# Summing the last 512 rows of w4 in four rows of 256 columns, with finer last loads and the output on another load semaphore

## The chip, the cores, the metric

The kernel runs on one core of a Trainium2 chip. The metric is the device time of one execution in microseconds (us). All quoted runs are "fast"; for a single core that only says that no run was over 1.5% above the fastest of its kernel. Times inside an execution are counted from its first instruction. The span of a profiled execution is about 1.8 us shorter than its time.

Engine names: PE is TensorE, DVE VectorE, ACT ScalarE, and SyncE issues most loads. PEld is PE's weight load.

## The reference

One decode step: grouped-query attention over a long cache plus a small gated MLP, in parallel, summed.

```python
# x: (1, 1, 1024); k_cache, v_cache: (1, 4, 65536, 128); wq, wo: 1024x4096, 4096x1024
# w1, w2: 1024x1024; w3: 1024x3584; w4: 3584x1024, all bf16
xn = layernorm(x)
A  = attention(xn @ wq, k_cache, v_cache) @ wo
h  = mix(gelu(layernorm(xn) @ w1)) @ w2
B  = xn + h + gelu(layernorm(xn + h) @ w3) @ w4     # S = 1, so the mix is a zero padding here
return x + A + B
```

(In the reference the shift by the mix leaves only zeros for one position, so the kernel feeds w3 from the same normed row.) Nearly all of the work is reading 170 MB.

## The kernel before

Loads go through eight hardware load semaphores in turn. The kernel sums every contribution to the output (x, each group's wo, w2, w4) in one PSUM bank `psB`: columns 0 to 511 in row 0, columns 512 to 1023 in row 32. The two rows lie in two 32-column strips of the PE array, so the two matmuls of a pair run side by side (in the trace they start 4 ns apart). w4 is the last weight; its last chunks are loaded in small pieces.

```python
W4_PIECES = ((8, 8), (8, 2, 1, 1))            # chunks of 128 rows, for the two tiles of w4
...
stream += [("wo", HKV - 1), ("V", NU - 1), ("w4", 0), ("w4", 1)]     # the last loads, in order
...
def row_acc(j, lhsT, rhs):                     # 1x512 into row 32*j of psB
    nc.tensor.matmul(psB[32 * j:32 * j + 1, :], lhsT=lhsT, rhs=rhs, start=False, stop=False,
                     tile_position=(0, 32 * j), skip_group_check=True)
...
def compute_w4(i, lo=0, hi=None): ...          # for each chunk, row_acc for j = 0 and 1
...
    compute_w4(0, W4_PIECES[0][0])
    compute_w4(1)
    out_t = ppool.tile([64, 512], BF16, name="out_t", tag="p_sb")
    nc.scalar.copy(out=out_t[:], in_=psB[0:64, :])
    nc.scalar.dma_start(out=out[0, 0, :].rearrange("(j n) -> j n", j=2),
                        in_=out_t[:].rearrange("(a b) n -> a b n", b=32)[:, 0, :])
```

## Time and profile before

405.86 us (median of 3, 405.73 to 405.91) when the prediction was made.

| event in the tail | us from the start |
|---|---|
| last V complete | 382.92 |
| w4 in pieces of 8, 8, 8 chunks complete | 387.80, 392.70, 397.59 |
| pieces of 2, 1, 1 chunks complete | 398.83, 399.48, 400.12 |
| last matmul ends | 400.54 |
| output copy on ACT | 400.58 to 401.16 |
| output lands | 402.86 |
| last instruction ends | 404.05 |

A load is complete when the last of the 16 DMA engines has counted up its semaphore; these moments are read from the trace's semaphore records. The table says that everything until 400.12 is the DMA stream, and 3.9 us of serial tail follow.

From the page of the kernel before, the span and, in 40 slices, the busy tenths of PE, the granted PE clock in tenths and the busy tenths of the DMA engines:

```profile
span 404.1 us, 3287 instructions
...
PE   0382727839483859292929394565658561948094
...
PEclk9998558688897979797978979596959895879769
DMA  8999999999999999999999999999999999999993
```

DMA is full from the second slice to the last but one; PE is not. From the chain of waits of the kernel before, its last pieces (start, duration, what):

```profile
355.04 42.55 DMA big<-in_B_w_dram
397.59 0.04 issue
397.63 2.93 PE psB L179 x24
400.56 0.02 issue
400.58 0.58 ACT out_t L526
```

From the timeline of the kernel before (start, duration, engine, line, operation, out<-in, shapes, count, idle before and its releaser):

```profile
397.63 2.91 PE L179 MATMUL psB<-big,cols_h 128*1 128x512 bf16 x24 [1.55 <-DMA big<-in_B_w_dram]
...
400.58 0.58 ACT L526 CAST out_t<-psB 64x512 bf16<-64x512 f32 x1 [25.40 <-PE psB L179]
401.19 0.61 ACTq L527 DMA_DIRECT2D out_dram<-out_t  x1
```

The chain puts the last 2.93 us down to PE, but these 24 matmuls hold one more real wait. PE starts a pair every 0.216 us from 397.63 on, and the small pieces of 2 and 1 chunks are there before it needs them. Only the last pair waits: it starts at 400.16, 0.04 us after the last load.

### The profile page before, as it was taken

To read this page: it belongs to the slowest core of one execution; us is meant where nothing else is said; L and a number is where in the kernel's file an instruction comes from. 1 tells how busy PE (TensorE), PEld (TensorE's weight loads), DVE (VectorE), ACT (ScalarE), POOL (GpSimd) and SP (SyncE) were. 2 spreads that over 40 slices of the span, in tenths; PEclk is the share of its full clock that TensorE was granted. 3 is DMA by queue.
4 is the path that set the end of the run, shared out by engine and by line. 5 is a ranking of instruction groups with operands and counts; after the bars stand their busy time and mean duration, and the time that the engine had idled before them with its cause. 6 is when DMAs were issued, how large, how long until landed. Compare 5 with 4: busy or idle time off the path is not lost.

```text
span 404.1 us, 3287 instructions
## 1 busy us (share of the span) xinstructions
PE 236.2 (58%) x1392; PEld 94.1 (23%) x1392; DVE 211.8 (52%) x241; ACT 34.3 (8%) x61; POOL 6.4 (2%) x19
## 2 busy tenths in 40 slices
PE   0382727839483859292929394565658561948094
PEld 0131202313131323031313231122213220313041
DVE  0310046957658584566585473738393934665310
ACT  1000210110101011001010101010101010010100
POOL 4000100000000000000000000000000000000000
PEclk9998558688897979797978979596959895879769
DMA  8999999999999999999999999999999999999993
GB/s 357 422 415 431 449 416 439 440 418 429 448 417 425 454 409 430 444 431 417 448 428 418 436 420 438 428 444 423 428 436 428 422 436 435 431 426 430 420 427 144
DMA packets 7237, 170.11 MB, mean 421 GB/s; under 512 B 1070, under 2 KB 1074, under 8 KB 1462
## 3 DMA queue, kind: packets, MB, share of 16 engines
q1 hardware_dynamic: 6912, 169.87, 98.1%
q8 instruction: 11, 0.18, 0.2%
q0 software_dynamic: 160, 0.02, 0.0%
q10 hardware_dynamic: 150, 0.01, 0.0%
q14 instruction: 4, 0.03, 0.0%
HBM read 169.88 MB, written 0.01 MB: 420 GB/s over the span
## 4 chain that ended last, share of the span: by engine, by line
DMA 49%; PE 30%; DVE 10%; another core or an unknown queue 6%; ACT 2%; issue 2%; SPq 0%; DVEq 0%; ACTq 0%
DMA big<-in_A_k_cache_dram 35%; PE sc L383 21%; DMA big<-in_B_w_dram 11%; DVE big L372 5%; PE oacc L457 4%; DMA x_bf<-in_A_x_dram 3%; DVE s_sb L390 2%; PE psq L250 1%; ACT p_sb L421 1%; PE psB L179 1%; PE psB L239 1%; DVE pT L424 1%; PE pm_mx L400 1%; DVE og L439 0%
## 5 line engine op out<-in xcount | busy, mean ns | idle before, releaser
L383 PE MATMUL sc<-big,qdiag 128*128 128x512 bf16 x512 | 150.0, 461 | 104.9 <-DVE big L372 104.9
L372 DVE STREAM_TRANSPOSE big<-big 128x2048 f32<-128x2048 f32 x64 | 142.4, 2279 | 49.4 <-DMA big<-in_A_k_cache_dram 49.4
L383 PEld LDWEIGHTS <-qdiag 128*128 128x128 bf16 x512 | 56.8, 111 | 193.2 <-issue 100.3
L457 PE MATMUL oacc<-big,pT 128*32 128x512 bf16 x512 | 37.7, 396 | 9.7 <-DMA big<-in_A_v_cache_dram 9.7
L390 DVE TENSOR_SCALAR_CACHE_REDUCE s_sb<-sc 128x1024 f32<-128x1024 f32 x16 | 19.6, 1225 | 45.0 <-PE sc L383 45.0
L424 DVE STREAM_TRANSPOSE pT<-p_sb 128x1024 bf16<-128x1024 bf16 x16 | 19.8, 1240 | 16.8 <-ACT p_sb L421 16.8
L463 ACT COPY ob<-oacc 128x512 f32<-128x512 f32 x12 | 7.0, 586 | 214.6 <-PE oacc L457 214.6
L421 ACT ACTIVATE p_sb<-s_sb,nball 128x1024 bf16<-128x1024 f32 x16 | 18.4, 1150 | 76.5 <-DVE nball L419 76.5
L457 PEld LDWEIGHTS <-pT 128*32 128x32 bf16 x512 | 14.0, 99 | 28.7 <-issue 17.1
L400 PE MATMUL pm_mx<-ident_f,mx 128*1 128x128 f32 x16 | 4.3, 270 | 16.7 <-DVE s_sb L390 16.7
L419 DVE COPY nball<-pm_mx 128x1 f32<-128x1 f32 x16 | 2.5, 153 | 17.5 <-PE pm_mx L413 17.5
L250 PE MATMUL psh<-big,ln_rep_b 128*32 128x512 bf16 x56 | 5.5, 505 | 8.8 <-DMA big<-in_B_w_dram 8.8
L466 DVE SCALAR_TENSOR_TENSOR og<-oacc,wb,og 128x512 f32<-128x512 f32 x4 | 3.0, 751 | 12.5 <-PE oacc L457 12.5
L179 PE MATMUL psB<-big,cols_h 128*1 128x512 bf16 x56 | 7.7, 420 | 1.6 <-DMA big<-in_B_w_dram 1.6
L189 PE MATMUL pm_ln<-ln_rowsum_a,ones_f 128*128 128x1 f32 x2 | 0.6, 348 | 13.7 <-DVE sel L213 13.7
L179 PE MATMUL psB<-w,oT 128*1 128x512 bf16 x64 | 7.6, 379 | 0.0
L473 PE MATMUL pm_e<-og,selbig 128*128 128x128 f32 x32 | 5.6, 326 | 3.2 <-DVE nball L419 2.3
L402 DVE TENSOR_REDUCE negm<-pm_mx 1x8 f32<-1x128 f32 x16 | 4.4, 275 | 5.4 <-PE pm_mx L400 5.4
L250 PEld LDWEIGHTS <-ln_rep_b 128*32 128x32 bf16 x72 | 3.4, 120 | 15.0 <-issue 12.2
L183 DVE CAST xT<-x_bf 128x8 f32<-128x8 bf16 x1 | 0.2, 172 | 12.0 <-DMA x_bf<-in_A_x_dram 12.0
L400 PEld LDWEIGHTS pm_mx<-ident_f,mx 128*1 128x1 f32 x16 | 1.3, 79 | 21.9 <-DVE s_sb L390 21.9
L439 DVE SCALAR_TENSOR_TENSOR og<-ob,wb,og 128x512 f32<-128x512 f32 x8 | 6.0, 751 | 0.1
(98 smaller groups left out, 80.5 us busy)
## 6 DMA issues: line engine op xcount, KB each, us to landing
big<-in_A_k_cache_dram SPq DMA_DIRECT2D x16, 4096.0 KB, 46.1
big<-in_A_v_cache_dram SPq DMA_DIRECT2D x16, 4096.0 KB, 39.9
big<-in_A_wq_dram SPq DMA_DIRECT2D x2, 4096.0 KB, 16.9
w<-in_A_wo_dram SPq DMA_DIRECT2D x4, 2048.0 KB, 30.1
big<-in_B_w_dram SPq DMA_DIRECT2D x2, 3584.0 KB, 34.3
big<-in_B_w_dram SPq DMA_DIRECT2D x3, 2048.0 KB, 40.7
w<-in_B_w_dram SPq DMA_DIRECT2D x2, 2048.0 KB, 42.6
big<-in_B_w_dram SPq DMA_DIRECT2D x1, 512.0 KB, 43.4
```

Of the source, the lines that this page charges most:

```text
L179: nc.tensor.matmul(psB[32 * j:32 * j + 1, :], lhsT=lhsT, rhs=rhs, start=False, stop=False, tile_position=(0, 32 * j), skip_group_check=True)
L250: nc.tensor.matmul(acc[i][32 * q:32 * q + 32], lhsT=rep[:, c, :], rhs=wt[:, k, 512 * s:512 * (s + 1)], start=first, stop=last, tile_positi ...
L372: nc.vector.transpose(out=words, in_=words)
L383: nc.tensor.matmul(sc[:, sub, :], lhsT=qdiag[:, c0:c0 + P], rhs=cols[:, sub, s, :, b, :, r], start=(s == 0 and b == 0 and r == 0), stop=(s ...
L390: nc.vector.tensor_scalar(out=s_sb[:], in0=sc[:], scalar1=SCALE, scalar2=None, op0=ALU.mult, op1=ALU.max, accum_out=mx[:])
L400: nc.tensor.transpose(pm[0:1, 0:P], unit.pop((u, "mx"))[:, 0:1], ident_f[:])
L421: nc.scalar.activation(out=p_sb[:], in_=unit.pop((u, "ssb"))[:], func=ACTF.Exp, bias=nball[:, b:b + 1], scale=1.0, accum_out=group[(g, "la ...
L424: nc.vector.transpose(out=pT[:].rearrange("p u n -> p (u n)"), in_=p_sb[:].rearrange("p u n -> p (u n)"))
L439: nc.vector.scalar_tensor_tensor(out=og[:], in0=ob[:], scalar=wb[:, k:k + 1], in1=og[:], op0=ALU.mult, op1=ALU.add)
L457: nc.tensor.matmul(oacc[32 * q:32 * (q + 1), :], lhsT=pT[:, sub, 32 * t:32 * (t + 1)], rhs=vt[:, sub, :, t, :], start=(sub == 0 and t < 4) ...
L463: nc.scalar.copy(out=ob[:], in_=oacc[:])
L473: nc.tensor.matmul(pe[:, 0:P], lhsT=selbig[:, cg, :], rhs=og[:, 128 * cg:128 * (cg + 1)], start=(cg == 0), stop=(cg == 3))
```

## The change

The intent: leave less to do after the last load. The sum of all but the last four chunks is copied out of `psB` (DVE), spread by four f32 matmuls with an identity over four rows of 256 columns (`psC`), and the last four chunks are added in four strips. The output copy is then 256 columns wide instead of 512. Loads near the end are split so that PE can start earlier; five more loads also shift the output to the eighth load semaphore, the last one that the end of the program waits for.

```diff
-W4_PIECES = ((8, 8), (8, 2, 1, 1))
+W4_PIECES = ((4, 4, 4, 4), (4, 4, 2, 1, 1))
+LAST = 4
 ...
-                nc.sync.dma_start(out=t[:], in_=wo_v[i] if src is None else src)
+                src = wo_v[i] if src is None else src
+                for lo, hi in ((0, 4), (4, 8)) if it == ("wo", HKV - 1) else ((0, 8),):
+                    nc.sync.dma_start(out=t[:, lo:hi], in_=src[:, lo:hi])
 ...
-                nc.sync.dma_start(out=t[:], in_=src)
+                n = UKEYS // SUBS if it == ("V", NU - 1) else UKEYS
+                for at in range(0, UKEYS, n):
+                    nc.sync.dma_start(out=t[:, at:at + n], in_=src[:, at:at + n])
 ...
+    def close_out():
+        acc = opool.tile([64, 512], F32, name="acc", tag="ob")
+        nc.vector.tensor_copy(out=acc[:], in_=psB[0:64, :])
+        psC = ps_O.tile([P, 512], F32, name="psC", tag="oacc")
+        for j in range(4):
+            nc.tensor.matmul(psC[32 * j:32 * j + 32, 0:256],
+                             lhsT=ident_f[0:64, 32 * (j // 2):32 * (j // 2) + 32],
+                             rhs=acc[:, 256 * (j % 2):256 * (j % 2 + 1)], start=True, stop=False, ...)
+        for k in (the last LAST chunks):
+            for j in range(4):
+                nc.tensor.matmul(psC[32 * j:32 * j + 1, 0:256], lhsT=vals["hT"][:, c:c + 1],
+                                 rhs=wt[:, 1024 * k + 256 * j:1024 * k + 256 * (j + 1)], ...)
+        return psC
 ...
-    compute_w4(1)
-    out_t = ppool.tile([64, 512], BF16, name="out_t", tag="p_sb")
-    nc.scalar.copy(out=out_t[:], in_=psB[0:64, :])
+    compute_w4(1, 0, sum(W4_PIECES[1]) - LAST)
+    psC = close_out()
+    out_t = ppool.tile([P, 256], BF16, name="out_t", tag="p_sb")
+    nc.scalar.copy(out=out_t[:], in_=psC[:, 0:256])
```

(Shortened; the output DMA writes four rows of 256.)

More of the change, by code (lines that the diff above doesn't have):

```diff
@@ L335, in compute_w2, with compute_w4 @@
         st.done(("w2", 0))
-    def compute_w4(i, lo=0, hi=None):
+    def compute_w4(i, lo, hi):
         wt = st.tiles[("w4", i)]
-        c0, n = sum(map(sum, W4_PIECES[:i])), sum(W4_PIECES[i])
-        hi = n if hi is None else hi
+        c0 = sum(map(sum, W4_PIECES[:i]))
         for k in range(lo, hi):
@@ L343, in compute_w4 @@
                 row_acc(j, vals["hT"][:, c0 + k:c0 + k + 1], wt[:, 1024 * k + 512 * j:1024 * k + 512 * (j + 1)])
-        if hi == n:
-            st.done(("w4", i))
+    def close_out():
[3 more added lines that the diff above has]
+        for j in range(4):
+            nc.tensor.matmul(psC[32 * j:32 * j + 32, 0:256], lhsT=ident_f[0:64, 32 * (j // 2):32 * (j // 2) + 32],
+                             rhs=acc[:, 256 * (j % 2):256 * (j % 2 + 1)], start=True, stop=False,
+                             tile_position=(0, 32 * j), skip_group_check=True)
+        wt = st.tiles[("w4", 1)]
+        for k in range(sum(W4_PIECES[1]) - LAST, sum(W4_PIECES[1])):
+            for j in range(4):
+                c = sum(W4_PIECES[0]) + k
+                nc.tensor.matmul(psC[32 * j:32 * j + 1, 0:256], lhsT=vals["hT"][:, c:c + 1],
+                                 rhs=wt[:, 1024 * k + 256 * j:1024 * k + 256 * (j + 1)], start=False, stop=(c == FC - 1),
+                                 tile_position=(0, 32 * j), skip_group_check=True)
+        return psC
     clock = [0]
@@ L451, in compute_v @@
         vt = st.tiles[("V", u)][:].rearrange("p (u s t d) -> p u s t d", u=SUBS, s=SETS, t=16)
-        oacc = ps_O.tile([P, 512], F32, name="oacc")
+        oacc = ps_O.tile([P, 512], F32, name="oacc", tag="oacc")
         pT = unit.pop((u, "pT"))
@@ L517 @@
             compute_v(i)
+    half = sum(W4_PIECES[0]) // 2
     while waiting:
@@ L520 @@
         if waiting:
-            compute_w4(0, 0, W4_PIECES[0][0])
-    compute_w4(0, W4_PIECES[0][0])
-    compute_w4(1)
-    out_t = ppool.tile([64, 512], BF16, name="out_t", tag="p_sb")
-    nc.scalar.copy(out=out_t[:], in_=psB[0:64, :])
-    nc.scalar.dma_start(out=out[0, 0, :].rearrange("(j n) -> j n", j=2),
+            compute_w4(0, 0, half)
+    compute_w4(0, half, 2 * half)
+    compute_w4(1, 0, sum(W4_PIECES[1]) - LAST)
+    psC = close_out()
+    out_t = ppool.tile([P, 256], BF16, name="out_t", tag="p_sb")
+    nc.scalar.copy(out=out_t[:], in_=psC[:, 0:256])
+    nc.scalar.dma_start(out=out[0, 0, :].rearrange("(j n) -> j n", j=4),
                         in_=out_t[:].rearrange("(a b) n -> a b n", b=32)[:, 0, :])
```

## The prediction

> **What bounds the kernel now.** The DMA stream. The page's 40 slices show DMA at 9 tenths from the second slice to the last but one (421 GB/s), while PE is busy 58% and DVE 52% of 404.1 us. The chain of waits ends with one DMA piece of 42.55 us (w4), then PE 2.93 us and ACT 0.58 us. So only the tail after the stream can change, and the stream's own length. In the trace's landing records the last V is complete at 382.92, the three big w4 pieces at 387.80, 392.70, 397.59, the small ones at 398.83, 399.48 and 400.12. After the last landing: two 1x512 matmuls end at 400.54, the 64x512 output copy on ACT takes 0.58 us, the output DMA's issue 0.61 us, it lands at 402.86 (1.69 us after the copy's end), SyncE then steps through five more semaphore waits (0.061 us each) before the end barrier; the span ends at 404.05.
>
> **What the change does, costed.**
> 1. Output semaphore: five more loads shift the output from the third load semaphore waited for to the eighth. The five waits after it disappear: -0.30 us, all on the critical path.
> 2. Output copy 128x256 instead of 64x512. ACT PSUM copies took 258 ns at 128 columns and 586 at 512, so 0.37 us (estimate) for 0.58: -0.21, on the path.
> 3. Five more DMAs. Landing intervals (9.72 us for 4 MB, 4.89 for 2 MB, 0.645 for 256 KB) leave 0.04 to 0.06 us per DMA, so the last landing moves to about 400.3. The late pieces now wait for an earlier load on their semaphore before issue, the last until about 385.5; about 6 MB are then still queued, so the stream doesn't run dry.
> 4. V and wo in halves: the last V's second half needs only 16 matmuls, so the group's end comes about 1.7 us sooner. PE had 1.55 us idle just before 397.63: off the path.
> 5. close_out is new and serial. The last piece before it lands at about 397.8; its eight 1x512 matmuls end near 398.85. DVE copies 64x512 f32 from PSUM: 0.69 us (q_row copy, same width). Then four f32 matmuls of 256 columns, two records each; an f32 record of 512 columns took 0.83 us at half clock, so 0.21 us at full clock. Neighbouring column strips overlapping, five slots: 1.1 us; serial: 1.7 us. The Trainium skill, "TensorEngine Tiling (Array Packing)", Key Properties, says different tiles execute in parallel; the trace agrees for bf16 (pairs of 1x512 matmuls start 4 ns apart), no run shows it for f32. f32 ends near 400.7 (or 401.3), after the last landing. The sixteen 1x256 matmuls wait behind it in order: four groups of 0.11 us and 0.17 us latency, end near 401.3 (401.9), against 400.54 before.
>
> So PE ends +0.75 (to +1.4) later, copy -0.21, waits -0.30: net about +0.25 to +0.9 us. PE's granted clock should be full there [...]; if it is half, another 1 us.
>
> **Prediction:** 406.2 us, 8 in 10 between 405.3 and 406.9. Faster by over 2%: 0.005; within 2%: 0.99; slower: 0.005.
>
> **What would show it right:** the last load landing near 400.3; PE not waiting for the last three pieces but for the DVE copy of psB; f32 matmuls spanning 1.1 to 1.7 us; ACT copy near 0.37 us starting after 401.2; no semaphore waits behind the output's.
>
> **What would make it wrong:** f32 matmuls overlapping fully or much cheaper, so the last landing is again what PE waits for (then about 405.4); an idle or cold PE in the tail; small pieces slowing the stream.

## The result, and the profile after

406.62 us (median of 4, 405.92 to 407.06), beside 405.81 (405.73 to 405.91) for the kernel before. Ratio 1.0018, 95% interval 1.0001 to 1.0036: the same within 2%. A ratio is the mean time of one kernel's fast runs over that of the other's of the same rounds, so it is not quite the ratio of the medians. The profiled run took 406.61 us.

From the page of the changed kernel, the lines that answer to those of before:

```profile
span 404.8 us, 3326 instructions
...
PE   0383526749465767293929384566566762838393
...
PEclk9997759979896969686868988596969695979577
DMA  8999999999999999999999999999999999999993
```

From its chain of waits, the last pieces:

```profile
373.24 24.70 DMA big<-in_B_w_dram
397.94 0.04 issue
397.98 1.05 PE psB L184 x8
399.03 0.02 issue
399.05 0.69 DVE acc L352
399.74 0.14 issue
399.88 0.98 PE psC L355 x8
400.86 0.98 PE psC L362 x16
401.84 0.02 issue
401.86 0.37 ACT out_t L548
```

From its timeline:

```profile
397.98 1.03 PE L184 MATMUL psB<-big,cols_h 128*1 128x512 bf16 x8 [1.46 <-DMA big<-in_B_w_dram]
...
399.05 0.68 DVE L352 COPY acc<-psB 64x512 f32<-64x512 f32 x1 [9.68 <-PE psB L184]
...
399.88 0.98 PE L355 MATMUL psC<-acc,ident_f 64*32 64x256 f32 x8 [0.87 <-DVE acc L352]
...
400.79 1.02 PE L362 MATMUL psC<-big,cols_h 128*1 128x256 bf16 x16
401.86 0.37 ACT L548 CAST out_t<-psC 128x256 bf16<-128x256 f32 x1 [25.98 <-PE psC L362]
402.26 0.62 ACTq L549 DMA_DIRECT2D out_dram<-out_t  x1
```

The DMA piece of the chain now ends at 397.94, not with the last load, which lands at 400.45. After it comes a serial chain: eight matmuls, DVE copy, f32 matmuls, sixteen matmuls. PE's last sixteen no longer wait for any load: they start at 400.79, when the last load has been there for 0.34 us.

The two traces' difference adds up. PE ends at 401.81 instead of 400.54: +1.27. The output copy takes 0.37 instead of 0.58: -0.21. From the output's landing to the end barrier there is one semaphore wait instead of six: -0.31. With +0.02 of small gaps that is +0.77, the difference of the spans (404.05 and 404.82).

The semaphore waits, from SyncE's records (not a view of the profile, but its instruction records: start and end in ns; the first wait of each kernel is for the output):

```
before  402872-402899  402936-402964  402997-403025  403057-403085  403118-403146  403177-403205  then the barrier at 403245
after   403950-403978  then the barrier at 404017
```

One more thing stands in the trace. The matmuls after 400.0 are slow for their size, and the view of windows shows why (window, length, busy us and count of PE, PEld, DVE, ACT, POOL, then the granted clock, DMA share and GB/s); changed kernel:

```profile
396.63:400.04 3.41, 1.19 (x12) 0.45 (x15) 0.68 (x1) 0.00 (x0) 0.00 (x0) 1.00 0.45 170
400.04:403.40 3.36, 1.77 (x24) 0.38 (x16) 0.00 (x0) 0.37 (x1) 0.00 (x0) 0.50 0.00 0
```

At 400.04 the clock fell to half, in the middle of the f32 matmuls, after a window in which PE had been busy for 1.19 of 3.41 us. In the trace of the kernel before, the window at this place holds more matmul work, and the clock stayed full:

```profile
395.20:398.62 3.42, 1.86 (x20) 0.69 (x16) 0.00 (x0) 0.00 (x0) 0.00 (x0) 1.00 0.68 261
```

(In both, the window's edges are those of the clock records, a whole number of 3.41 us from each change of the clock.) So three theories were put to the test:

- **S (serial):** the new close (copy, f32 matmuls, sixteen matmuls behind them) is longer than the 2.5 us that the remaining loads give it.
- **L (loads):** the finer loads delay the stream, and that costs the time.
- **C (clock):** the close fits or nearly fits at full clock, and the fall to half clock costs the time.

### The profile page after: what moved, and what is told of

Same layout as the page of the kernel before. It is cut to its first block, busy times and chain, and to the rows that moved or that the text cites. A ratio compares the mean times of both kernels' runs of the same rounds, so it can differ in the third digit from the quotient of the medians.

```text
span 404.8 us, 3326 instructions
## 1 busy us (share of the span) xinstructions
PE 235.8 (58%) x1408; PEld 94.0 (23%) x1408; DVE 213.0 (53%) x242; ACT 34.1 (8%) x61; POOL 6.3 (2%) x19
## 4 chain that ended last, share of the span: by engine, by line
DMA 58%; PE 25%; DVE 9%; another core or an unknown queue 6%; ACT 1%; issue 1%; SPq 0%; ACTq 0%
DMA big<-in_A_k_cache_dram 38%; PE sc L403 16%; DMA w<-in_A_wo_dram 10%; DMA big<-in_B_w_dram 6%; DVE big L392 4%; DMA x_bf<-in_A_x_dram 3%; PE oacc L477 3%; DVE s_sb L410 2%; PE psq L255 2%; PE psB L184 1%; PE psB L244 1%; ACT p_sb L441 1%; DVE og L459 1%; PE pm_mx L420 0%
## 5 line engine op out<-in xcount | busy, mean ns | idle before, releaser
L403 PE MATMUL sc<-big,qdiag 128*128 128x512 bf16 x512 | 147.5, 454 | 109.7 <-DVE big L392 109.5
L255 PE MATMUL psh<-big,ln_rep_b 128*32 128x512 bf16 x56 | 7.1, 623 | 6.4 <-DMA big<-in_B_w_dram 6.3
L255 PE MATMUL psq<-big,ln_rep_a 128*32 128x512 bf16 x64 | 6.2, 576 | 0.0
```

What stands on the lines that cost most here:

```text
L255: nc.tensor.matmul(acc[i][32 * q:32 * q + 32], lhsT=rep[:, c, :], rhs=wt[:, k, 512 * s:512 * (s + 1)], start=first, stop=last, tile_positi ...
L403: nc.tensor.matmul(sc[:, sub, :], lhsT=qdiag[:, c0:c0 + P], rhs=cols[:, sub, s, :, b, :, r], start=(s == 0 and b == 0 and r == 0), stop=(s ...
```

## The experiments

Every kernel here gave a correct result. On the chips used, the kernel before itself scattered more than at first: 406.20 (405.69 to 408.16, 11 runs) beside the first four experiments, 406.89 (405.81 to 407.40, 11 runs) beside the next four and 406.49 (405.81 to 407.40, 12 runs) beside the last four, on the same chip as those before. Eleven of these twelve are the same runs that stand beside the four experiments before; only one, 405.96, is new. So absolute times and traces are compared first, ratios second.

| run | median (range) | ratio to before (95%) | last load | last matmul ends |
|---|---|---|---|---|
| before, first trace | 405.81 (405.73 to 405.91) | - | 400.12 | 400.54 |
| the change, first trace | 406.62 (405.92 to 407.06) | 1.0018 (1.0001 to 1.0036) | 400.45 | 401.81 |
| finer loads alone | 405.97 (405.89 to 406.69) | 0.9992 (0.9972 to 1.0012) | 400.53 | 400.95 |
| tiny loads at the start | 408.72 (407.97 to 409.69) | 1.0055 (1.0033 to 1.0076) | 402.46 | 404.09 |
| change, LAST = 8 | 405.66 (405.49 to 405.86) | 0.9980 (0.9962 to 0.9997) | 400.57 | 400.89 |
| change, PE kept busy | 405.99 (405.88 to 406.08) | 0.9988 (0.9970 to 1.0005) | 400.52 | 401.14 |
| the change again | 406.21 (405.80 to 406.80) | 0.9992 (0.9974 to 1.0010) | 400.52 | 401.53 |
| close with coarse loads | 406.73 (406.64 to 408.28) | 1.0016 (0.9996 to 1.0036) | 400.04 | 401.48 |
| LAST = 8, coarse, tiny loads last | 406.00 (405.69 to 406.24) | 0.9986 (0.9971 to 1.0001) | 400.74 | 401.06 |
| before, tiny loads last | 405.73 (405.65 to 406.96) | 0.9985 (0.9967 to 1.0002) | 400.07 | 402.00 |
| before, PE kept busy | 406.01 (405.77 to 406.21) | 0.9986 (0.9969 to 1.0003) | 400.26 | 400.69 |
| the same, tiny loads last | 405.76 (405.69 to 405.86) | 0.9981 (0.9965 to 0.9998) | 400.27 | 400.70 |
| the same, four rows from the start | 405.53 (405.46 to 405.64) | 0.9975 (0.9960 to 0.9990) | 400.42 | 400.75 |
| LAST = 8 again | 405.70 (405.37 to 405.93) | 0.9978 (0.9963 to 0.9993) | 400.36 | 400.68 |

The last two columns are of the one profiled run of each, which is not always a typical one ("tiny loads last": 406.96 us, the others 405.65 to 405.78).

### Finer loads alone

```diff
-    psC = close_out()
-    ... copy of psC[:, 0:256], four rows
+    compute_w4(1, 0, sum(W4_PIECES[1]))
+    ... copy of psB[0:64, :], two rows, as before
```

> Finer loads and the output semaphore that comes with them, without the new summation (output from two rows of 512 as before). Theory S (the serial close of copy, f32 matmuls and sixteen matmuls ends the kernel): last load lands near 400.45 as in the changed kernel, two matmuls 0.42 us, copy 0.58, five waits fewer (-0.31): 405.7 to 406.1 us, little scatter. Rival L (the finer loads cost the time): about 406.6 us. Rival C (half clock in the tail is the cost): as S, because little matmul work is left after the last load.

405.97 us. The tail of its timeline:

```profile
400.57 0.38 PE L184 MATMUL psB<-big,cols_h 128*1 128x512 bf16 x2 [0.26 <-DMA big<-in_B_w_dram]
...
400.99 0.58 ACT L547 CAST out_t<-psB 64x512 bf16<-64x512 f32 x1 [25.59 <-PE psB L184]
```

PE waits for the last load again. The finer loads move that load by about a third of a microsecond (the six traces with all of them have it at 400.36 to 400.57, mean 400.49; the five with the loads of before, and at most tiny ones behind them, have it at 400.04 to 400.27, mean 400.15; four rows from the start, with its extra instruction fetch, is left out), and the semaphore gives 0.31 back. L falls as an explanation of 0.8 us: the loads and the semaphore together cost about 0.1 (spans 404.05 and 404.14). Not all went as expected: two of the six runs, 406.43 and 406.69, lie above 405.7 to 406.1. No trace of such a run exists, so their cause is open.

### LAST = 8

```diff
-LAST = 4
+LAST = 8
```

> The changed kernel with LAST = 8: the same operations, but the sum so far is taken over one piece (2.5 us) earlier, so copy and f32 matmuls end near 398.3, before the last load lands (400.45). S: PE ends 0.3 to 0.6 us after the last load, 405.4 to 405.9 us. L: stays near 406.6, the loads are the same. C: stays between 406 and 407 with the same scatter, the clock being as before (PE is no busier).

405.66 us, every run below 405.9. The same operations, one piece earlier:

```profile
396.68 0.68 DVE L352 COPY acc<-psB 64x512 f32<-64x512 f32 x1 [7.18 <-PE psB L184]
...
397.50 0.64 PE L355 MATMUL psC<-acc,ident_f 64*32 64x256 f32 x8 [0.87 <-DVE acc L352]
...
400.61 0.28 PE L362 MATMUL psC<-big,cols_h 128*1 128x256 bf16 x4 [0.36 <-DMA big<-in_B_w_dram]
...
400.94 0.37 ACT L548 CAST out_t<-psC 128x256 bf16<-128x256 f32 x1 [25.70 <-PE psC L362]
```

Copy and f32 matmuls now end near 398.1, and the last four matmuls wait for the last load and end 0.32 us after it. The close costs next to nothing when it stands where PE has time. This is what S says. L, which had the time stay near 406.6 because the loads are the same, is refuted. So is C as it was put here, 406 to 407. This run does not test a milder C: in its trace the clock fell at 402.04 only, after the last matmul.

### PE kept busy

Ten matmuls into a PSUM row that nobody reads: six before the second piece of four chunks of the last tile, four while DVE copies.

```diff
+    def keep_warm(n, c):
+        idle = ps_M.tile([P, 512], F32, name="idle", tag="pm")
+        for k in range(n):
+            nc.tensor.matmul(idle[0:1, :], lhsT=vals["hT"][:, 0:1], rhs=<half of chunk c of w4(1)>, start=True, stop=True, ...)
 ...
+    compute_w4(1, 0, 4)
+    keep_warm(6, 3)
-    compute_w4(1, 0, sum(W4_PIECES[1]) - LAST)
+    compute_w4(1, 4, sum(W4_PIECES[1]) - LAST)
 ... in close_out, behind the DVE copy:
+        keep_warm(4, 7)
```

> The changed kernel with ten extra 1x512 matmuls into an unused PSUM row: six in the gap before the second four-row piece of w4(1) lands, four while DVE copies psB. They only keep PE busy. C: granted clock stays 1.0 in the tail, f32 part near 0.6 us and the last sixteen matmuls near 0.7 us instead of 0.98 and 1.02; 405.7 to 406.1 us in every run, scatter under 0.3 us. S without clock: unchanged near 406.6, scatter about 1 us as in the changed kernel.

405.99 us, all six runs within 0.20. Its timeline and its windows:

```profile
399.13 0.68 DVE L358 COPY acc<-psB 64x512 f32<-64x512 f32 x1 [9.69 <-PE psB L184]
...
399.96 0.64 PE L362 MATMUL psC<-acc,ident_f 64*32 64x256 f32 x8
...
400.53 0.61 PE L369 MATMUL psC<-big,cols_h 128*1 128x256 bf16 x16
401.19 0.37 ACT L557 CAST out_t<-psC 128x256 bf16<-128x256 f32 x1 [26.22 <-PE psC L369]
```

```profile
394.70:398.11 3.41, 2.79 (x19) 0.90 (x17) 0.00 (x0) 0.00 (x0) 0.00 (x0) 1.00 0.87 340
398.11:401.50 3.39, 3.01 (x36) 1.02 (x35) 0.68 (x1) 0.32 (x1) 0.00 (x0) 1.00 0.13 48
```

More work made the kernel faster: with PE busy 2.79 of 3.41 us the clock stays full, the f32 part takes 0.64 us instead of 0.98 and the last sixteen 0.61 instead of 1.02. Against the change's first trace the span is 0.68 us shorter (404.82 and 404.14). C holds for most of the difference. It does not hang on where the clock's windows happened to lie: of all stretches of 3.41 us that end between 394.0 and the last matmul, the emptiest has PE busy for 82% in this trace, and for 30% in the change's first trace (worked out from the matmul records). What is left belongs to S: PE still ends 0.62 us after the last load (401.14 and 400.52) where LAST = 8 needs 0.32.

### The change again

The changed kernel unaltered, for a second trace.

> The changed kernel, unaltered, for a second trace and on the same chip as the three below. C and S together: the tail's length follows from when the clock falls to half. If it falls before the sixteen last matmuls (400.0 in the first trace), they take 1.0 us and the run 406.5 to 407.1; if the clock stays full to their end, f32 0.64 us, last matmuls 0.6 us and the run 405.8 to 406.1. Median 406.2 to 406.7.

406.21 us, 405.80 to 406.80. Windows, and the two PE groups of the close:

```profile
397.15:400.56 3.41, 1.64 (x20) 0.49 (x23) 0.68 (x1) 0.00 (x0) 0.00 (x0) 1.00 0.33 124
400.56:403.97 3.41, 0.97 (x19) 0.34 (x16) 0.00 (x0) 0.37 (x1) 0.00 (x0) 0.50 0.00 1
```

```profile
399.94 0.64 PE L355 MATMUL psC<-acc,ident_f 64*32 64x256 f32 x8 [0.87 <-DVE acc L352]
...
400.51 1.02 PE L362 MATMUL psC<-big,cols_h 128*1 128x256 bf16 x16
```

Here the fall came 0.5 us later, between the two groups: f32 at full clock, the sixteen at half, and a profiled run of 406.32. The three traces (fall at 400.04: 406.61; at 400.56: 406.32; no fall: 405.94) order as C says.

### Close with coarse loads

The change with `W4_PIECES = ((8, 8), (8, 2, 1, 1))` and V and wo loaded whole.

> The new summation with the loads of before (w4 in 8, 8, 8, 2, 1, 1, V and wo whole; output on the third semaphore). S: the sum so far is only complete after sixteen matmuls that start at the landing near 397.6, so the DVE copy starts near 399.5, half a microsecond later than with finer loads; last matmul near 401.6 at full clock, plus five semaphore waits: 406.5 to 407.1 us, 407.5 at half clock. L (finer loads are the cost): 405.5 to 405.9 us.

406.73 us at the median. The DVE copy starts at 399.47 instead of 399.05, the last load lands at 400.04, and PE ends at 401.48 with the clock full to the end (the sixteen took 0.61), where the change with PE kept busy ended at 401.14. So within the change the finer loads bring the close forward by 0.34 us, and the later last load that they cause does not end that kernel. The rest of this run's loss against it is the five semaphore waits. L's 405.5 to 405.9 is ruled out once more. Two of the six runs took 408.2; no trace of such a run exists, and their cause is open. Half clock is a candidate, as PE idles for 3.02 us before its sixteen matmuls here.

### Tiny loads: the semaphore alone

To move only the output's semaphore, five loads of 32 bytes were added to the kernel before. First at the start of the program:

```diff
     nc.scalar.dma_start(out=x_row[:], in_=A_x[0, 0:1, :])
+    pad = const.tile([1, 5, 16], BF16, name="pad")
+    for k in range(5):
+        nc.scalar.dma_start(out=pad[0:1, k, :], in_=A_x[0, 0:1, 16 * k:16 * k + 16])
```

> The kernel before, with five tiny loads of 32 bytes added at the start, which only shift the output to the load semaphore that is waited for last. All theories: five waits of 0.061 us fall away, 405.4 to 405.65 us against 405.8 (-0.3), copy and last load as before. If the time stays at 405.8, the semaphore part of the change is worth nothing.

A miss, by three microseconds: 408.72. The first 20 us of the kernel before, then of this one, in the view of windows:

```profile
0.00:20.00 20.00, 3.19 (x8) 1.69 (x8) 4.29 (x30) 1.75 (x3) 4.76 (x16) 1.00 0.94 394
```

```profile
0.00:20.00 20.00, 3.35 (x8) 1.68 (x8) 4.29 (x30) 1.75 (x3) 4.76 (x16) 1.00 0.85 341
```

DMA moved 341 instead of 394 GB/s in that stretch; 53 GB/s over 20 us is 1.06 MB, or 2.5 us of the stream, and the last load came 2.34 us later. The trace shows why. From SyncE's waits in the first 60 us of this kernel:

```profile
SPq L132 <- DMA x_bf<-in_A_x_dram: 11.9, 1, 11.9
```

The five tiny loads took the next five semaphores, so the second big load came round to the semaphore that the load of `x_bf` still held. SyncE issued it at 13.00 us instead of 1.17, and from 12 to 16 us DMA moved 206 GB/s, where in the kernel before it moved 460. So it is not the tiny loads' own semaphores that the big load waits for. The run tells nothing of the output's semaphore.

Then behind the last w4 load, on SyncE:

> The kernel before plus five 32-byte loads issued behind its last w4 load, for the output's semaphore alone; the earlier attempt put them at the start and slowed the first loads' issue. Five waits of 0.061 us fall away, nothing else moves: 405.4 to 405.65 us with the output's landing to the end barrier 0.09 us instead of 0.39. If the tiny loads land after the output's semaphore is ready, no gain: 405.8 or more.

Five of six runs took 405.65 to 405.78, just above the expected 405.4 to 405.65. The sixth, which is the profiled one, took 406.96, and is the most useful miss:

```profile
397.56 4.44 PE L183 MATMUL psB<-big,cols_h 128*1 128x512 bf16 x24 [2.02 <-DMA big<-in_B_w_dram]
...
402.04 0.58 ACT L530 CAST out_t<-psB 64x512 bf16<-64x512 f32 x1 [27.32 <-PE psB L183]
```

```profile
394.24:397.65 3.41, 1.39 (x16) 0.51 (x12) 0.00 (x0) 0.00 (x0) 0.00 (x0) 1.00 0.87 342
397.65:401.06 3.41, 3.41 (x18) 1.12 (x16) 0.00 (x0) 0.00 (x0) 0.00 (x0) 0.50 0.17 64
```

Its last load came early, at 400.07. But the clock fell at 397.65, and the 24 matmuls that took 2.91 us in the kernel before took 4.44. This is the tail of the kernel before: it, too, has a slow form, in which PE and not DMA ends last.

### The kernel before, with PE kept busy

```diff
+    keep_warm(7, 0, 15)          # seven 1x512 matmuls on the last chunk of w4(0), before the last tile's matmuls
     compute_w4(1)
```

(The edit also drops `st.done` for w4, as the change does, so that the tile can still be read; no load is left to be issued then.)

> The kernel before with seven extra 1x512 matmuls into an unused PSUM row, in PE's gap before the piece of eight chunks that lands near 397.6. C (the clock's free-running windows make the scatter of the kernel before: in the run of the tail loads its tail fell to half clock at 397.65 and the last 24 matmuls took 4.4 us instead of 2.9): all six runs 405.7 to 406.0, while the unaltered kernel beside it scatters up to 407 or more. Rival D (the scatter is the DMA's: last load later in slow runs): scatter stays above 1 us.

405.77 to 406.21 in six runs, where the kernel before went to 407.40 on the same chip. No long run came, as C says; the remaining scatter of 0.44 is a little above the expectation. But all of those long runs were taken with the four experiments before, so it is not shown that the kernel before would have had them in these rounds too, and D (late loads) is less firmly refuted than the numbers look. The traces speak for C more directly: the emptiest stretch of 3.41 us, as above, has PE busy for 41% in the twin with tiny loads last, which fell to half, for 54% in the kernel before, and for 87% here. For the kernel before's own long runs there is no trace, so their cause is made likely by its twin and by this run, and not shown directly.

### Candidates for a faster version

Three more kernels tried to beat both.

LAST = 8, coarse loads but for one split, and four tiny loads last:

> Candidate for a faster version: LAST = 8, only the second w4 tile's first eight chunks halved, all other loads as before, and four 32-byte loads behind the last w4 load so that the output stays on the semaphore waited for last. S: last load 0.2 to 0.35 us sooner than with all finer loads, otherwise as LAST = 8 (405.66): 405.3 to 405.5 us. L's weaker form (loads cost nothing each): 405.6 to 405.8.

406.00, a miss: not faster than LAST = 8 with all finer loads; its last load came at 400.74, later than with all of them. Why is open.

The kernel before with PE kept busy and five tiny loads last:

> The same with five 32-byte loads behind the last w4 load for the output's semaphore. C and the semaphore's five waits: 405.4 to 405.75 in all six runs, about 0.2 to 0.3 us under the one without them.

405.76, just above what was expected for all six runs (405.69 to 405.86), and 0.25 below the same without the tiny loads (406.01). This is the semaphore's 0.3, measured on its own.

The same, with every partial sum kept in four rows of 256 columns from the start (`row_acc` for j in 0 to 3, 256 columns each), so that the narrow copy needs no close:

> As the last, with every partial sum kept in four rows of 256 from the start, so that the output copy is 128x256 without any close_out. S: last matmul 0.3 us after the last load, copy 0.37 us: 405.1 to 405.5. Against it: 272 more PE instructions need a twelfth instruction fetch of 16 KB[...]; if it meets the slowest engine, 405.7 to 406.2.

405.53, all six runs within 0.18: the lowest median and the least but one scatter, though the twelfth instruction fetch did come (in its packets by queue, twelve of 16 KB where the kernel before has eleven; each held one DMA engine for 0.93 to 1.11 us) and its last load came at 400.42. Last matmul 0.32 us after the last load, as expected; the time is just above the 405.1 to 405.5 of S.

LAST = 8 with all finer loads, on the same chip:

> LAST = 8 with all finer loads once more, for the comparison with the three above on one chip: 405.5 to 405.9 us in all runs, as at its first run (405.66); its last loads have only four groups of 256 columns behind each, so the clock's phase should hardly show.

405.70. One more edit of one number would have made the change a small gain: ratio 0.9978 (0.9963 to 0.9993), and four rows from the start 0.9975 (0.9960 to 0.9990). Their intervals do not tell the two apart. Both ratios are taken beside the kernel before with its long runs; beside the kernel before with PE kept busy (406.01) LAST = 8 gains 0.3 us.

## Why the prediction was right, and where its steps were off

The predicted time was 406.2 us, 405.3 to 406.9; measured 406.62. In this comparison the direction held, and so did the mechanism of a serial close; two terms were off with opposite signs, so the nearness of the number is in part luck.

1. **The DMA stream bounds the kernel, only the tail can change:** right. The DMA line of the page is the same in both.
2. **Semaphore, -0.30:** right. -0.31 between the two traces, 0.25 between two kernels that differ in it alone.
3. **Narrow copy, 0.37 for 0.58:** right, 0.37.
4. **Last load near 400.3:** a little small; 400.45. The stream did not run dry.
5. **V and wo in halves off the path:** right as to the earlier end. The group's last V matmuls end 1.7 us sooner (DVE follows at 385.02 instead of 386.71) and PE then waits for w4.
6. **The close is serial and ends after the last load:** right in kind. "f32 ends near 400.7 (or 401.3), after the last landing" came true at 400.86. But the term "Neighbouring column strips overlapping, five slots: 1.1 us; serial: 1.7 us" was mis-sized: with the clock full the eight f32 records take 0.64 us. They come in two bunches: four start within 0.02 us, and four more follow 0.25 us later within 0.1 us, as this list of the changed kernel's f32 records shows (start and duration in ns, half clock from 400040 on):

```
399878 458   399886 517   399892 524   399899 530
400132 631   400198 631   400211 632   400224 632
```

   The page of the Trainium skill that the prediction cited, "TensorEngine Tiling (Array Packing)", section Key Properties, says that different tiles execute in parallel; the trace agrees for f32 as for bf16. The prediction reckoned with five slots one after the other; the records show two. Which record belongs to which strip the trace does not say.
7. **"PE's granted clock should be full there":** this is the step that failed. It fell at 400.04 in the first trace and at 400.56 in the second. The prediction named the case ("if it is half, another 1 us"), and it cost 0.68 us of span (404.82 against 404.14 with PE kept busy). The trace on hand could have warned it: there the clock fell 17 times, always after a window with PE busy for at most 32%, and stayed full only with 46% or more, and the close leaves PE idle while DVE copies. The prediction did not work out how busy that leaves PE (35% in the window before the fall). The Trainium skill, "TensorE: Matmul & The Clock Gate", Part 1, says that the clock is set by a free-running window of 3413 ns; the traces agree, as every fall and rise lies a whole number of 3.41 us from the others of its run (kernel before: 378.14, 391.79, 405.44). The page names "≥1 idle window" as what lowers the clock. The measurement differs: here a window with PE busy for 1.19 of 3.41 us was enough.

So, against the prediction's lower branch (f32 in 1.1 us, net +0.25 us), the f32 term was about 0.46 us too long and the clock's 0.68 was left out; the piece before the sum landed 0.14 later than said (397.94 for 397.8), and from the DVE copy to the f32 matmuls it took 0.15, not the 0.06 that followed the q_row copy in the kernel before. Together that is +0.45: 405.86 + 0.25 + 0.45 is 406.56, beside 406.61 of the profiled run. An error of 0.46 and one of 0.68 stood against each other, and that is luck. Of the signs named as proof, the last load, the DVE copy, the ACT copy and the missing waits showed as said; the f32 span of 1.1 to 1.7 us did not. The sentence on what would make it wrong was half right: the f32 matmuls did overlap fully, yet PE did not wait for the last load again, because the piece before the sum lands only 2.5 us earlier.

And the comparison itself was luckier for the kernel before than it looked. In its first four runs no slow tail occurred. In the later runs it had many long ones, and beside those the unaltered change stood at 0.9992 (0.9974 to 1.0010). Half clock cost the change about 0.7 us; the tail of the kernel before, in its twin with tiny loads last, lost 1.2 (406.96 against 405.73).

## What to carry to other kernels

Before moving work behind a partial sum, ask which load completes that sum and how long the rest of the stream lasts after it: here the same close was a loss when its sum was complete 2.5 us before the last load, and nearly free when it was complete 5 us before. In a tail where PE waits for loads, look at the granted clock window by window; a stage with PE less than half busy can fall to half clock. Here a few useless matmuls (0.68 us) were then worth more than the narrower copy (0.21 us). When one kernel's runs scatter, read a trace of a slow one before explaining a difference of a few tenths.

## What the Trainium skill lacked or had wrong

- "TensorE: Matmul & The Clock Gate", Part 1 and "Why this matters for your kernels": the clock is said to fall after an idle window, and idle gaps over about 3 us are warned of. (Its passage on a second failure mode does tell of the clock swinging through short idle times, but gives no figure for how little work is enough.) In fourteen traces it fell 267 times: 262 times after windows in which PE was busy for up to 48%, and five times, all near 31 us, after 53 to 57% (worked out from the clock and matmul records). It stayed full 675 times, with 43% busy at the least, so between 43 and 57% both happened. In the tail of the change it fell with no gap over 1.46 us.
- The same page, same part: the rise after a window of sustained work agrees; it rose (256 times) only after windows that were 75% busy or more. But it also stayed at half after some windows of up to 91%.
- "TensorEngine Tiling (Array Packing)": names FP32 only with transpose mode, and gives no time for f32 matmuls on column strips. Four f32 matmuls of 256 columns on four strips took 0.64 us together at full clock; eight records start in two bunches.
- "DMA: Bandwidth & Descriptors", on the anatomy of one DMA: gives a fixed cost of a single software-path DMA, about 2 us, but not what one more load costs inside a full stream. Here a load of 2 MB took 4.89 us from landing to landing, two of 1 MB 2 x 2.485: 0.08 us for one more. Five more moved the last load by 0.34 us on the mean of the traces above.
- No page found: the end of the program waits for the load semaphores one after the other, 0.061 us each, so an output on the last of them saves up to seven; five were measured as 0.31 us. And small loads at the start moved a big load onto a semaphore still in use, which cost 2.3 us of the stream in one experiment.
